# Router logits of seven chunks as multiply-and-sum on VectorE in place of flips and products on TensorE

## The chip, the cores and the metric

The kernel runs on one core of a Trainium2 chip. The metric is the device time of one execution in microseconds (us). TensorE (PE in the profile), VectorE (DVE), ScalarE (ACT), GpSimd (POOL) and SyncE (SP) each follow an instruction stream of their own and wait for each other by semaphores.

## The reference

Three layers in a row over 2304 tokens of 512 features, all in float32:

```python
scores = q @ k.T / 8 + bias            # 4 x 8 heads, causal, window of 128 tokens
x = softmax(scores) @ v                # attention
x = (h * clip(h + 3, 0, 6) / 6) @ w_out, with h = x @ w_in      # hard-swish layer
xn = x / (norm(x) + 1e-6)              # router
en = emb / (norm(emb) + 1e-6)          # 8 embeddings of 512
logits = xn @ en.T / tau
e = argmax(logits);  gate = softmax(logits)[e]
out = gate * (relu(x @ w1[e]) @ w2[e])                           # one expert per token
```

The change is in `logits` alone: eight sums of products of 512 per token.

## The kernel before, in words

The tokens go through attention and the hard-swish layer in nine chunks (`c`, 0 to 8) of 256, two tiles of 128 rows each. Attention runs in units of one chunk and one pair of heads, four units to a chunk; chunks 0 and 1 are `Early` units, the others `Unit`s. A `Unit` transposes its loaded keys and queries on VectorE (`kT`, `qT`, L567), scores them on TensorE (`sc_ps`, L583), finds the row limits and masks on VectorE (`soften`, L593 to L599), takes the exponential on ScalarE, scales on VectorE (`normalise`, L608 to L612), flips the weights on TensorE (`ps_pt`, L618), copies and masks them on ScalarE and GpSimd (`ph`, L625, L633) and multiplies by the values on TensorE (`acc`, L644). The attention of a chunk runs about two chunks ahead of its hard-swish layer.

The hard-swish layer of a chunk goes in eight steps `i` of 256 hidden features. Each has 24 products into `h_ps` (`gemm1`, L676), then `u` on ScalarE and VectorE (L686, L693), its split into `gh` on ScalarE and `gl` on VectorE (L155, L156), then 12 products into `y_ps` (`gemm2`, L719); products are made in three passes of split operands. In the chunks from 2 on, one step takes 1.91 of the planner's units of time, so a chunk takes 15.28.

When the last step of chunk `c` is done, its class `Route` begins: `rows` copies `y_ps` to two tiles `ys` and stores them; `flip` transposes each (`ps_y`, L747, 4 transposes a tile) and copies it to `yT` (L749); `norms` squares and sums the rows on ScalarE, in place, and takes a root on GpSimd (`rn`, L759); `logits` multiplies by the transposed embeddings `enT` (`lgT`, L766) and copies (L771); `total` adds the four parts (`lg`, L776); `choose` finds the expert on VectorE (L787 to L797); `ranks` counts earlier tokens of the same expert (`rk`, L802, L803); `place` computes a slot per token and scatters the row numbers to `slots` by two indirect DMAs on GpSimd (L818). After chunk 8 the experts run, with rows gathered by those slots.

The order of the work is fixed by `at(step, fn)`: all calls are sorted by their planned step, and TensorE executes its instructions in just that order. On the other engines a scheduler sorts the calls' instructions, and each engine then runs them in that order. SP issues nearly all loads and stores, one queue in order; the small loads `kr` and `qr` of keys and queries (L538) are 16 issues a unit. The pool `wp` has 17 buffers of 8 KB per partition; from the time that the weights of the hard-swish layer are all there, 16 of them hold these. The pool tag `f` has five buffers of 128x512.

The table `ROUTE` gives the steps of a chunk's `flip`, `norms`, `logits` and `ranks`, counted from the end of its last `gemm2`; its first row holds for chunks 0 to 6, its second for chunk 7. Chunk 8 has a schedule of its own.

Of the kernel before, what the change touches and what calls it, by code (L numbers as in the profile page):

```python
# [9 lines left out]
F32 = mybir.dt.float32  # L10
# [3 lines left out]
AF = mybir.ActivationFunctionType  # L14
ALU = mybir.AluOpType
# [42 lines left out]
P_BUFS, V_BUFS = 2, 2  # L58
FLIPS_AHEAD = 0.01

ROUTE = ((3.76, 4.57, 6, 8.46), (1, 1.43, 2.92, 4.5))

TOTAL = 0.95
PLACE_0 = (6.5, 10.6, 6.7, 2.08, 2.2, 1.0, 8.6)
# [27 lines left out]
def tile_kernel(  # L92
# [13 lines left out]
    nc = tc.nc  # L106
    B, H, S, D = q.shape
    NT, DM = out.shape
    DFF = w_in.shape[1] // 2
    NE = w1.shape[0]  # L110
# [3 lines left out]
    NCH = NT // CH  # L114
# [10 lines left out]
    dram = ctx.enter_context(tc.tile_pool(name="dram", bufs=1, space=bass.MemoryType.DRAM))  # L125
    main = ctx.enter_context(ExitStack())
    keep = main.enter_context(tc.tile_pool(name="keep", bufs=2))
    wp = main.enter_context(tc.tile_pool(name="wp", bufs=17))
# [8 lines left out]
    V = nc.vector  # L137

    def two_k(name, shape=(128, 512), dt=F32):
        return keep.tile(list(shape), dt, tag="f", bufs=5, name=name)  # L140

    def small(name, shape, dt=F32, bufs=2):
        return keep.tile(list(shape), dt, tag=name, bufs=bufs, name=name)
# [15 lines left out]
    def unit_of(head):  # L159
# [17 lines left out]
        out=whole, in_=whole, compare_op=ALU.is_ge, fill=MASKED, base=128, pattern=[[-1, 256]], channel_multiplier=1  # L177
    )
    nc.gpsimd.affine_select(
        out=whole, in_=whole, compare_op=ALU.is_ge, fill=MASKED, base=-1, pattern=[[1, 256]], channel_multiplier=-1  # L180
# [3 lines left out]
    for kinds in ((2, 2), (2, 0), (2, 1), (1, 2), (0, 2)):  # L184
        tables[kinds] = t = const.tile([128, 192], BF16, name="table%d%d" % kinds)
        for h, kind in enumerate(kinds):
            r = slice(64 * h, 64 * h + 64)
# [3 lines left out]


    ybuf = dram.tile([ROWS, DM], F32, name="ybuf")
    slots = dram.tile([NE * SLOTS, 2], I32, name="slots")

    pays = const.tile([128, NCH, 2, 2], I32, name="pays")
# [9 lines left out]
    units_of, half, share = fixed[:, 0:NP], fixed[:, NP:NP + 2], fixed[:, NP + 2:NP + 3]  # L206
# [7 lines left out]
        out=earlier, in_=earlier, compare_op=ALU.is_gt, fill=0.0, base=0, pattern=[[1, 128]], channel_multiplier=-1  # L214
# [5 lines left out]
        out=fold, in_=ident.rearrange("p (g e) -> p e g", g=KD)[:, 0:NE, :], axis=AX.X, op=ALU.add  # L220
# [38 lines left out]
    def embed():  # L259
        en = en_t.pop()[0:NE]  # L260

        junk = two_k("junk")
        n2 = small("n2", (NE, 1))
        nc.scalar.activation(out=junk[0:NE], in_=en, func=AF.Square, accum_out=n2)
        nc.gpsimd.tensor_tensor(out=n2, in0=n2, in1=half[0:NE, 0:1], op=ALU.pow)
        V.scalar_tensor_tensor(out=n2, in0=n2, scalar=1e-6, in1=rtau[0:NE], op0=ALU.add, op1=ALU.mult)
        V.reciprocal(out=n2, in_=n2)
        V.tensor_scalar(out=en, in0=en, scalar1=n2, scalar2=None, op0=ALU.mult)
        en_t.append(en)

    def turn_embed():
# [456 lines left out]
    class Route:  # L728
# [3 lines left out]
        def rows(self):  # L732
            c = self.c
            self.ss = small("ss", (128, 2))
            self.ys = []
            for t in range(2):
                ys = two_k("ys")
                nc.scalar.activation(out=ys, in_=y_t[c][t], func=AF.Copy, scale=1.0 / 6.0)
                r0 = c * CH + t * 128
                nc.sync.dma_start(out=ybuf[r0:r0 + 128, :], in_=ys)  # L740
                self.ys.append(ys)
            self.pay = pays[:, c]
# [11 lines left out]
        def norms(self):  # L754
            for t in range(2):
                ys = self.ys[t]
                nc.scalar.activation(out=ys, in_=ys, func=AF.Square, accum_out=self.ss[:, t:t + 1])
            self.rn = rn = small("rn", (128, 2))
            nc.gpsimd.tensor_tensor(out=rn, in0=self.ss, in1=half, op=ALU.pow)  # L759

        def logits(self):

            ps = bank([128, CH], "lgT")
            for t in range(2):
                for kk in range(KD):
                    nc.tensor.matmul(  # L766
                        ps[32 * kk:32 * kk + 32, t * 128:(t + 1) * 128], lhsT=enT[:, kk, :], rhs=self.yT[t][:, kk, :],
                        start=True, stop=True, skip_group_check=True,
                    )
            self.lgT = small("lgT", (128, CH), bufs=1)  # L770
            nc.scalar.copy(self.lgT, ps)  # L771
# [140 lines left out]
    def fetch(j, t):  # L912
        o, n = tiles_of(j)[t]
        xg = two_k("xg")
        ids, src = ids_t[j][0:n, t, 0:1], ybuf
        if j == 0 and o < EARLY:
            src = ybuf[0:NT - CH + 1, :]
            if t == 0:
                rows_t.append(small("rows", (128, n_first), I32))
            rows = rows_t[0][0:n, t:t + 1]  # L920
            V.tensor_scalar(out=rows, in0=ids, scalar1=NT - CH, scalar2=None, op0=ALU.min)
            ids = rows
        nc.gpsimd.indirect_dma_start(  # L923
            out=xg[0:n], out_offset=None, in_=src, in_offset=bass.IndirectOffsetOnAxis(ap=ids, axis=0)
        )
        xg_t[j, t] = xg
# [152 lines left out]
    def at(step, fn, *args):  # L1079
        todo[step].append((fn, args))  # L1080

    def begins(c, i=0):
        return FIRST_1[i] if c == 1 else FIRST[0] + FIRST[1] * (8 * (c - 2) + i)
# [5 lines left out]
    def ends(c, i=NF2 - 1):  # L1089
        return 0.0 if c == 0 else begins(c, i) + (SECOND_1 if c == 1 else FIRST[2])  # L1090
# [138 lines left out]
            at(begins(c, i), split_g, c, i)  # L1229
    for n in range(0, NT // 128, 3):  # L1230
        at(begins(BLANK[0] + n // 3, BLANK[1]), blank, n, n + 3)
    at(ROUTE[0][0] - 3.0, embed)
    at(ROUTE[0][0] - 0.3, turn_embed)
    for c in range(NCH - 1):
        r = Route(c)
        g = ends(c)
        d = ROUTE[c == NCH - 2]
        assert 0 < d[0] <= d[1] <= d[2] < d[2] + TOTAL < d[3]
        at(g, r.rows)
        at(g + d[0], r.flip, 0)  # L1240
        at(g + d[1], r.flip, 1)
        at(g + d[1], r.norms)
        at(g + d[2], r.logits)
        at(g + d[2] + TOTAL, r.total)
        at(g + d[2] + TOTAL, r.choose)
        at(g + d[3], r.ranks)
        at(g + d[3], r.place)
    g = begins(NCH - 1)
# [3 lines left out]
        pools["x"] = main.enter_context(tc.tile_pool(name="x2", bufs=1, side="right"))  # L1252

    at(g - 1, close_attention)
    assert g + PLACE_0[0] > ends(NCH - 2) + ROUTE[1][3]
    at(g + PLACE_0[0], rank_experts, False)
    at(g + PLACE_0[0], load_order, False, 0)
    at(g + PLACE_0[6], load_ids, 0, range(n_first))
# [9 lines left out]
    g = ends(NCH - 1)  # L1268
# [8 lines left out]
    r = Route(NCH - 1)  # L1277
# [14 lines left out]
    late = (n_first,)  # L1292
# [19 lines left out]
    for j in range(1, NE):  # L1312
# [6 lines left out]
        if j == 1:  # L1319
            s = PLACE_1  # L1320
            loads = [s[0] + s[1] * i for i in range(4)]
            splits = [s[2] + s[3] * i for i in range(8)]
            ids, gets, turns = LATE[0] + 0.05, [s[4] + s[5] * t for t in range(n)], [s[8] + s[9] * t for t in range(n)]
        else:
            s = [x + b - 16 for x in NEXT]
            s[5], s[7], s[9] = NEXT[5], NEXT[7], NEXT[9]
            loads = [s[0], s[1], s[2], s[3]]
# [39 lines left out]
    with tc.If(n_rounds > 0):  # L1367
        with ExitStack() as rest:
# [15 lines left out]
            def overflow(j, r):  # L1384
# [16 lines left out]
                for n in range(NT // 128):  # L1401
                    rows = f2.tile([128, DM], F32, tag="rows", name="rows_r")
                    nc.sync.dma_start(out=rows, in_=ybuf[n * 128:(n + 1) * 128, :])
                    hot = f2.tile([128, 128], F32, tag="hot", name="hot")
                    V.tensor_scalar(
                        out=hot, in0=wanted, scalar1=-128.0 * n, scalar2=down_p, op0=ALU.add, op1=ALU.is_equal
                    )
                    for kk in range(KD):
                        nc.tensor.matmul(
                            ps[:, kk, :], lhsT=rows[:, kk * 128:(kk + 1) * 128], rhs=hot,  # L1410
                            start=(n == 0 and kk == 0), stop=(n == NT // 128 - 1 and kk == KD - 1),
                            skip_group_check=True,
                        )
# [19 lines left out]
                for n in range(NT // 128):  # L1433
                    rows = f2.tile([128, DM], I32, tag="rows", name="rows_r")
                    nc.sync.dma_start(out=rows, in_=out[n * 128:(n + 1) * 128, :].bitcast(I32))
                    hot = f2.tile([128, 128], F32, tag="hot", name="hot")
                    V.tensor_scalar(
                        out=hot, in0=across, scalar1=128.0 * n, scalar2=whose, op0=ALU.add, op1=ALU.is_equal
                    )
                    moved = pf.tile([128, DM], F32, tag="moved", name="moved")  # L1440
                    nc.tensor.matmul(moved, lhsT=hot, rhs=ob, start=True, stop=True)
                    theirs = pf.tile([128, DM], F32, tag="theirs", name="theirs")
                    nc.tensor.matmul(theirs, lhsT=hot, rhs=all_one, start=True, stop=True)
                    mine = f2.tile([128, DM], I32, tag="mine", name="mine")
                    V.tensor_copy(out=mine, in_=theirs)
                    V.copy_predicated(rows, mine, moved.bitcast(I32))
                    nc.sync.dma_start(out=out[n * 128:(n + 1) * 128, :].bitcast(I32), in_=rows)
# [35 lines left out]
```

## Time and profile before

| what | value |
|---|---|
| median of 3 runs (lowest, highest) | 789.95 us (789.27, 791.37) |
| profiled execution: its own time | 795.89 us |
| profiled execution: span from first to last instruction | 793.9 us |
| mean granted clock of TensorE in it | 0.992 of full speed |
| TensorE busy | 769.2 us, 97% of the span |
| VectorE busy | 454.7 us, 57% |
| ScalarE busy | 400.5 us, 50% |
| GpSimd busy | 177.1 us, 22% |
| attention and hard-swish layer, to chunk 8's end | about the first 575 us |
| experts | the rest |

The profiled execution is one of its own, 5.94 us (0.75%) above the median of the runs. Times within the trace are counted from the start of the span. Busy shares over the whole span mix stages: VectorE, for example, has slices at nine tenths in the first 100 us and slices at four to six tenths later. Matmuls are pipelined, so that rows of a TensorE timeline overlap, and what a group costs in a full stream is read from its start to the next group's start.

### The profile page before, as it was taken

The page shows a single profiled execution, that of the slowest core. Times are in us where ns is not written, and L with a number is a line of the kernel's source. Part 1 is how long each engine was busy: PE and PEld are TensorE (multiplying, and loading weights), DVE is VectorE, ACT ScalarE, POOL GpSimd, SP SyncE. Part 2 cuts the span into 40 slices and gives each one's busy share as a digit, 9 for nine tenths or more (in the row PEclk, how much of TensorE's full clock was granted, in tenths as well). Part 3 has the DMA queues.
Part 4 walks back from the last instruction along what each step waited for, and adds up shares of the span by engine and source line. Part 5 has one row for each costly group of instructions (what it writes and reads, how often), then busy time and mean ns, then how long its engine had stood idle before and what let it go on. Part 6 is the DMA issues. An engine that isn't in the chain of part 4 may idle for free. (4 is left out here: it accounts for less than half of the span.)

```text
span 793.9 us, 16238 instructions
## 1 busy us (share of the span) xinstructions
PE 769.2 (97%) x5970; PEld 677.6 (85%) x5970; DVE 454.7 (57%) x1272; ACT 400.5 (50%) x941; POOL 177.1 (22%) x357
## 2 busy tenths in 40 slices
PE   7999999999999999999999999999989999999995
PEld 5666577788888898898988888888989999999994
DVE  2799987656565555646456453237827537546621
ACT  5898655455454454455454452426525535544510
POOL 4000003222221312313232322013123122133210
PEclk9999999999999999999999999999999999999998
DMA  9954522422333232242323110048268465456200
GB/s 258 338 179 111 176 49 48 54 61 47 77 80 78 39 67 74 37 96 46 74 61 59 52 52 1 28 93 294 94 206 269 149 219 194 149 201 216 82 26 27
DMA packets 157077, 88.51 MB, mean 111 GB/s; under 512 B 119187, under 2 KB 135699, under 8 KB 156992
## 3 DMA queue, kind: packets, MB, share of 16 engines
q1 hardware_dynamic: 153248, 77.84, 35.9%
q0 software_dynamic: 3744, 9.58, 3.5%
q8 instruction: 49, 0.80, 0.5%
q14 instruction: 36, 0.29, 0.2%
HBM read 73.03 MB, written 14.46 MB: 110 GB/s over the span
## 5 line engine op out<-in xcount | busy, mean ns | idle before, releaser
L676 PEld LDWEIGHTS h_ps<-xs,w_i 128*128 128x128 f32 x1536 | 192.1, 192 | 6.4 <-issue 2.0
L676 PE MATMUL h_ps<-xs,w_i 128*128 128x256 f32 x1536 | 196.1, 284 | 0.0
L719 PE MATMUL y_ps<-w_o,gh 128*128 128x512 f32 x512 | 163.5, 400 | 1.0 <-ACT gh L155 0.9
L686 ACT ACTIVATE u<-h_ps,three 128x512 f32<-128x512 f32 x72 | 49.4, 687 | 126.4 <-PE h_ps L676 101.3
L719 PEld LDWEIGHTS y_ps<-w_o,gh 128*128 128x128 f32 x512 | 91.5, 188 | 24.8 <-issue 7.0
L633 POOL TENSOR_SCALAR_AFFINE_SELECT ph<-ph 64x128 f32<-64x128 f32 x224 | 78.1, 349 | 141.3 <-ACT ph L625 88.7
L693 DVE SCALAR_TENSOR_TENSOR u<-u,h_ps 128x512 f32<-128x512 f32 x72 | 49.4, 685 | 104.3 <-ACT u L686 103.9
L965 PE MATMUL ps_u<-x,w_e 128*128 128x280 f32 (+5 forms) x768 | 105.0, 293 | 0.0
L719 PE MATMUL y_ps<-w_o,gl 128*128 128x512 f32 x256 | 100.5, 393 | 0.4 <-DVE gl L156 0.4
L965 PEld LDWEIGHTS ps_u<-x,w_e 128*128 128x128 f32 x768 | 100.2, 188 | 0.2
L156 DVE TENSOR_TENSOR w_e<-st,w_e 128x1024 fp32r<-128x1024 f32 x64 | 76.5, 1217 | 38.2 <-ACT w_e L155 38.2
L989 PE MATMUL ps_o<-hs,w_e 128*128 128x280 f32 (+4 forms) x576 | 79.9, 299 | 0.0
L989 PEld LDWEIGHTS ps_o<-hs,w_e 128*128 128x128 f32 x576 | 78.0, 192 | 0.0
L155 ACT CAST w_e<-st 128x1024 fp32r<-128x1024 f32 x64 | 65.5, 1049 | 17.1 <-DMA st<-in_moe_w_dram 6.2
L156 DVE TENSOR_TENSOR gl<-u,gh 128x512 fp32r<-128x512 f32 x64 | 45.8, 715 | 37.1 <-ACT gh L155 37.1
L602 ACT ACTIVATE pt<-pt,nm 128x128 f32<-128x128 f32 x112 | 44.1, 394 | 31.3 <-DVE pt L599 29.9
L719 PEld LDWEIGHTS y_ps<-w_o,gl 128*128 128x128 f32 x256 | 48.0, 188 | 12.0 <-DVE gl L156 1.5
L1064 POOL DMA_INDIRECT out_dram<-ob,ids x23 | 30.3, 1317 | 116.4 <-DVE ob L1063 105.9
L155 ACT CAST gh<-u 128x512 fp32r<-128x512 f32 x64 | 39.6, 619 | 22.3 <-DVE u L693 22.2
L973 ACT ACTIVATE hs<-ps_u 128x280 fp32r<-128x280 f32 (+5 forms) x64 | 25.6, 403 | 44.9 <-PE ps_u L965 44.2
L974 DVE SCALAR_TENSOR_TENSOR hs<-ps_u,hs 128x280 fp32r<-128x280 f32 (+5 forms) x64 | 27.9, 442 | 20.1 <-ACT hs L973 19.8
L818 POOL DMA_INDIRECT slots<-pays,dest x18 | 19.9, 1104 | 84.6 <-DVE u L693 52.1
(180 smaller groups left out, 1021.6 us busy)
## 6 DMA issues: line engine op xcount, KB each, us to landing
st<-in_moe_w_dram SPq DMA_DIRECT2D x32, 512.0 KB
st<-in_moe_w_dram SPq DMA_DIRECT2D x16, 1024.0 KB
wst<-in_moe_w_in_dram SPq DMA_DIRECT2D x8, 1024.0 KB
wst<-in_moe_w_out_dram SPq DMA_DIRECT2D x8, 1024.0 KB
ybuf<-ys SPq DMA_DIRECT2D x18, 256.0 KB
out_dram<-empty SPq DMA_DIRECT2D x18, 256.0 KB
kr<-in_k_dram SPq DMA_DIRECT2D x48, 48.0 KB
vr<-in_v_dram SPq DMA_DIRECT2D x24, 96.0 KB
```

Source lines behind the costliest of these rows:

```text
L155: nc.scalar.copy(hi, src)
L156: eng.tensor_tensor(out=lo, in0=src, in1=words(hi), op=ALU.subtract)
L602: nc.scalar.activation(out=x, in_=x, func=AF.Exp, scale=-1.0, bias=nm[:, j:j + 1], accum_out=sums[h][:, j:j + 1])
L633: nc.gpsimd.affine_select(out=out, in_=x, compare_op=ALU.is_gt if out is prev else ALU.is_ge, fill=0.0, base=0, pattern=[[0, 2], [-1 if ou ...
L676: nc.tensor.matmul(hp[:, f, :], lhsT=w[:, a, kk, f * 128:(f + 1) * 128], rhs=xs[:, b, kk, :], start=(n == 0), stop=(n == 3 * KD - 1),)
L686: nc.scalar.activation(out=u, in_=hp, func=AF.Relu, bias=three, scale=1.0)
L693: V.scalar_tensor_tensor(out=u, in0=u, scalar=6.0, in1=h_t[c, i], op0=ALU.min, op1=ALU.mult)
L719: nc.tensor.matmul(y_t[c][t], lhsT=g[a][:, f, t * 128:(t + 1) * 128], rhs=w[:, b, f, :], start=(i == 0 and f == 0 and n == 0), stop=(i == ...
L965: nc.tensor.matmul(ps, lhsT=w[:, a, kk, (f % 2) * 128:(f % 2) * 128 + 128], rhs=x[:, b, kk, c0:c1], start=(n == 0), stop=(n == 3 * KD - 1),)
L974: V.scalar_tensor_tensor(out=hs[:, 1, f, c0:c1], in0=ps, scalar=0.0, in1=words(hs[:, 0, f, c0:c1]), op0=ALU.max, op1=ALU.subtract)
L989: nc.tensor.matmul(ps, lhsT=ws_t[j, 4 + f // 2][:, a, f % 2, d * 128:(d + 1) * 128], rhs=hs[:, b, f, 0:width(j)], start=(n == 0), stop=(n ...
L1064: x = nc.gpsimd.indirect_dma_start(out=out, out_offset=bass.IndirectOffsetOnAxis(ap=ids[0:n, t, 0:1], axis=0), in_=ob[0:n], in_offset=None ...
```

## The change

For chunks 0 to 6 `flip`, `logits` and `total` are no longer called. The eight normalised embeddings are written once to `en_rows` in DRAM. Per chunk, two loads (`spread`, 1 MB each) copy four of them to every partition, into the free buffer of `wp`, under the name `en_all`; both go through the same buffer one after the other, and both are on SP. `dots` then makes one `tensor_tensor_reduce` per embedding and tile on VectorE, 16 a chunk: `ys` times the embedding, elementwise, with the sum along the row into `lg`, and the products into a tile `junk` that nothing reads. `norms` puts its squares into the same `junk`, since `ys` must live on, and comes right after `rows`. `choose`, `ranks` and `place` follow at 10.9 and 12.28 steps after the chunk's end, where it was 6.95 and 8.46. Chunk 0's part is 4.0 steps later than the others'. `enT` is still made, for chunks 7 and 8, which are as before.

```diff
-ROUTE = ((3.76, 4.57, 6, 8.46), (1, 1.43, 2.92, 4.5))
+ROUTE = (1, 1.43, 2.92, 4.5)
+DOTS = ((-3.5, 4.5), (0.8, 1.0), (7.4, 0.8), 10.9, 12.28)
+EMBED = 4.0
...
+    en_rows = dram.tile([NE, DM], F32, name="en_rows")
...
         V.tensor_scalar(out=en, in0=en, scalar1=n2, scalar2=None, op0=ALU.mult)
+        nc.sync.dma_start(out=en_rows, in_=en)
...
         def norms(self):
             for t in range(2):
                 ys = self.ys[t]
-                nc.scalar.activation(out=ys, in_=ys, func=AF.Square, accum_out=self.ss[:, t:t + 1])
+                to = self.junk if self.c < NCH - 2 else ys
+                nc.scalar.activation(out=to, in_=ys, func=AF.Square, accum_out=self.ss[:, t:t + 1])
...
+        def spread(self, half):
+            self.en = wp.tile([128, NE // 2, DM], F32, tag="w", name="en_all")
+            src = en_rows[NE // 2 * half:NE // 2 * (half + 1), :].rearrange("(o e) d -> o (e d)", o=1)
+            nc.sync.dma_start(out=self.en.rearrange("p e d -> p (e d)"), in_=src.to_broadcast([128, NE // 2 * DM]))
+
+        def dots(self, e):
+            if e == 0:
+                self.lg = small("lg", (128, 2, NE))
+            for t in range(2):
+                V.tensor_tensor_reduce(
+                    out=self.junk, in0=self.ys[t], in1=self.en[:, e % (NE // 2), :],
+                    scale=1.0, scalar=0.0, op0=ALU.mult, op1=ALU.add, accum_out=self.lg[:, t, e:e + 1],
+                )
...
-    at(ROUTE[0][0] - 3.0, embed)
-    at(ROUTE[0][0] - 0.3, turn_embed)
+    at(EMBED - 3.0, embed)
+    at(EMBED - 0.3, turn_embed)
...
-        d = ROUTE[c == NCH - 2]
+        at(g, r.rows)
+        if c < NCH - 2:
+            at(g + 0.3, r.norms)
+            loads, *halves, d2, d3 = DOTS
+            late = EMBED if c == 0 else 0.0
+            for x in range(2):
+                at(g + loads[x] + late if c or x else 2.0, r.spread, x)
+            for e in range(NE):
+                x, y = divmod(e, NE // 2)
+                at(g + halves[x][0] + halves[x][1] * y + late, r.dots, e)
+            at(g + d2 + late, r.choose)
+            at(g + d3 + late, r.ranks)
+            at(g + d3 + late, r.place)
+            continue
+        d = ROUTE
```

How the instructions stand in the two programs is shown at three places. The first is TensorE in the hard-swish layer of chunk 3, where chunk 2's logits were made; `h_ps` and `y_ps` are the two products of the layer. Before:

```order
L719 MATMUL y_ps<-w_o,gl 128x512
L766 MATMUL lgT<-yT,enT 32x128 x8
L676 MATMUL h_ps<-xs,w_i 128x256 x24
L776 MATMUL lg<-fold,lgT 128x8 x2
L719 MATMUL y_ps<-w_o,gh 128x512 x2
L719 MATMUL y_ps<-w_o,gl 128x512
```

Now:

```order
L723 MATMUL y_ps<-w_o,gh 128x512 x2
L723 MATMUL y_ps<-w_o,gl 128x512
L680 MATMUL h_ps<-xs,w_i 128x256 x24
L723 MATMUL y_ps<-w_o,gh 128x512 x2
L723 MATMUL y_ps<-w_o,gl 128x512
```

`lgT` and `lg` are gone and nothing stands in their place; the two groups of flips before them are gone in the same way, and `rk` stands later, again right ahead of a `ps_pt`.

The second place is VectorE in the same chunk, in the attention unit beside the second half of chunk 2's dots. `pt` and `rs` are the unit's weights and row scales; a dot is the row L777 with `junk`, followed by a row that reads the sum out. Before, from the last L593 of the unit's `soften` to the end of its `normalise`:

```order
L593 ISA pt,nm<-sc_ps,table_100 128x192
L593 ISA nm 128x1
L567 STREAM_TRANSPOSE kT<-kr 128x384
L599 TENSOR_TENSOR pt<-pt 128x2x64
L608 TENSOR_SCALAR rs<-sums_150 128x2
L567 STREAM_TRANSPOSE qT<-qr 128x256
L609 RECIPROCAL rs<-rs 128x2
L612 TENSOR_SCALAR pt<-pt,rs 128x128 x2
```

Now:

```order
L777 ISA junk,lg<-ys,en_all 128x512
L777 ISA lg 128x1
L603 TENSOR_TENSOR pt<-pt 128x2x64
L612 TENSOR_SCALAR rs<-sums_151 128x2
L777 ISA junk,lg<-ys,en_all 128x512
L777 ISA lg 128x1
L613 RECIPROCAL rs<-rs 128x2
L571 STREAM_TRANSPOSE kT<-kr 128x384
L616 TENSOR_SCALAR pt<-pt,rs 128x128 x2
L612 TENSOR_SCALAR rs<-sums_152 128x2
```

Of the eight dots of this half, one stands ahead of the first half of `normalise`, one inside it and one inside the second half; the other five stand after it, two ahead of the next `u`, two between `u` and `gl` and one behind `gl`.

The third place is VectorE in chunk 1's hard-swish layer, beside the first half of chunk 0's dots. Before, across a unit's `soften` and `normalise`:

```order
L599 TENSOR_TENSOR pt<-pt 128x2x64
L608 TENSOR_SCALAR rs<-sums_150 128x2
L609 RECIPROCAL rs<-rs 128x2
L612 TENSOR_SCALAR pt<-pt,rs 128x128 x2
L813 TENSOR_TENSOR to<-rk,oh 128x16
L816 TENSOR_TENSOR seen<-seen,oh 128x8
```

Now, at the same unit, from `soften`'s last row on:

```order
L603 TENSOR_TENSOR pt<-pt 128x2x64
L777 ISA junk,lg<-ys,en_all 128x512
L777 ISA lg 128x1
L697 SCALAR_TENSOR_TENSOR u<-u,h_ps 128x512
L777 ISA junk,lg<-ys,en_all 128x512
L777 ISA lg 128x1
L612 TENSOR_SCALAR rs<-sums_151 128x2
L612 TENSOR_SCALAR rs<-sums_152 128x2
```

Three dots stand ahead of these rows, within `soften`, and three more behind them, two of them behind a `gl`, before the first `L616` of `normalise`: eight dots in all, together with a `u` and a `gl`, which stood behind `normalise` before. Chunk 0's `choose`, which stood ahead of this unit's `soften`, has moved behind the second half of the dots. That half stands in the same way around the `soften` and `normalise` of the unit after the next: eight dots, a `u` and a `gl`, and there a `kT` too, ahead of the last rows of `normalise`.

## Rows read from the trace of the kernel before

**Rows 1.** The page, busy time of each engine over the span:

```profile
PE 769.2 (97%) x5970; PEld 677.6 (85%) x5970; DVE 454.7 (57%) x1272; ACT 400.5 (50%) x941; POOL 177.1 (22%) x357
```

**Rows 2.** Busy by stretch: PE, PEld, DVE, ACT, POOL; then clock, DMA share, GB/s:

```profile
103.50:155.00 51.50, 49.28 (x427) 41.30 (x426) 35.63 (x137) 29.15 (x84) 13.47 (x36) 0.97 0.32 52
238.00:293.50 55.50, 55.50 (x495) 49.06 (x494) 31.30 (x121) 27.44 (x78) 14.27 (x36) 1.00 0.32 63
```

**Rows 3.** Timeline of TensorE: start, duration, engine, line, operation, count:

```profile
182.48 0.60 PE L747 MATMUL ps_y<-ident,ys 128*128 128x128 f32 x4
...
216.85 0.60 PE L618 MATMUL ps_pt<-ident,pt 128*128 128x128 f32 x4
...
230.20 0.60 PE L618 MATMUL ps_pt<-ident,pt 128*128 128x128 f32 x4
...
232.19 0.73 PE L719 MATMUL y_ps<-w_o,gh 128*128 128x512 f32 x2
...
237.92 0.60 PE L747 MATMUL ps_y<-ident,ys 128*128 128x128 f32 x4
238.28 0.71 PE L719 MATMUL y_ps<-w_o,gh 128*128 128x512 f32 x2
...
249.39 0.64 PE L766 MATMUL lgT<-yT,enT 128*32 128x128 f32 x16
249.97 3.14 PE L676 MATMUL h_ps<-xs,w_i 128*128 128x256 f32 x24
252.95 0.51 PE L776 MATMUL lg<-fold,lgT 128*128 128x8 f32 x4
253.31 0.71 PE L719 MATMUL y_ps<-w_o,gh 128*128 128x512 f32 x2
...
273.00 0.89 PE L644 MATMUL acc<-ph,vr 64*64 64x192 f32 x24
...
460.43 0.60 PE L747 MATMUL ps_y<-ident,ys 128*128 128x128 f32 x4
```

**Rows 4.** Groups of VectorE by line and shape: busy, mean ns, idle before:

```profile
L156 DVE TENSOR_TENSOR gl<-u,gh 128x512 fp32r<-128x512 f32 x64 | 45.8, 715 | 37.1 <-ACT gh L155 37.1
L320 DVE SCALAR_TENSOR_TENSOR w<-wst,w 128x1024 int32<-128x1024 int32 x16 | 19.4, 1218 | 0.1
L458 DVE CUSTOM_DVE_ANT_0 pt<-sc_ps,table 128x256 f32<-128x256 f32 x24 | 9.3, 417 | 0.0
```

**Rows 5.** Timeline of VectorE in a unit without routing; in brackets the idle time before:

```profile
220.23 0.34 DVE L593 CUSTOM_DVE_ANT_0 pt<-sc_ps,table 128x192 f32<-128x192 f32 x1
...
221.97 0.57 DVE L567 STREAM_TRANSPOSE kT<-kr 128x384 f32<-128x384 f32 x1
...
224.14 0.48 DVE L612 TENSOR_SCALAR pt<-pt,rs 128x128 f32<-128x128 f32 x2
225.56 0.69 DVE L693 SCALAR_TENSOR_TENSOR u<-u,h_ps 128x512 f32<-128x512 f32 x1 [0.93 <-ACT u L686]
```

**Rows 6.** Timeline of TensorE in chunk 1's layer:

```profile
129.60 3.12 PE L676 MATMUL h_ps<-xs,w_i 128*128 128x256 f32 x24
...
135.83 0.73 PE L719 MATMUL y_ps<-w_o,gh 128*128 128x512 f32 x2
...
138.97 0.60 PE L618 MATMUL ps_pt<-ident,pt 128*128 128x128 f32 x4
...
152.31 3.63 PE L676 MATMUL h_ps<-xs,w_i 128*128 128x256 f32 x24
...
161.40 0.60 PE L618 MATMUL ps_pt<-ident,pt 128*128 128x128 f32 x4
```

**Rows 7.** Timeline of GpSimd behind a chunk's scatter:

```profile
270.20 2.44 POOL L633 TENSOR_SCALAR_AFFINE_SELECT ph<-ph 64x128 f32<-64x128 f32 x7 [6.81 <-DMA slots<-pays,dest]
```

**Rows 8.** Timeline of SP's queue, the issues of one unit's queries:

```profile
207.44 7.29 SPq L538 DMA_DIRECT2D qr<-in_q_dram  x8
```

More of the change, by code (lines that the diff above doesn't have):

```diff
@@ L735, in rows @@
             self.ys = []
+            if c < NCH - 2:
+                self.junk = two_k("junk")
             for t in range(2):
@@ L1236, in tile_kernel @@
         g = ends(c)
-        d = ROUTE[c == NCH - 2]
+        at(g, r.rows)
+        if c < NCH - 2:
+            at(g + 0.3, r.norms)
[11 more added lines that the diff above has]
+        d = ROUTE
         assert 0 < d[0] <= d[1] <= d[2] < d[2] + TOTAL < d[3]
-        at(g, r.rows)
         at(g + d[0], r.flip, 0)
@@ L1254, in tile_kernel @@
     at(g - 1, close_attention)
-    assert g + PLACE_0[0] > ends(NCH - 2) + ROUTE[1][3]
+    assert g + PLACE_0[0] > ends(NCH - 2) + ROUTE[3]
     at(g + PLACE_0[0], rank_experts, False)
```

## The prediction

> **What bounds the kernel now.** I read the busy shares first: TensorE is at 97% of the span, VectorE at 57%, ScalarE at 50%, GpSimd at 22% [rows 1]. Then the table of busy time by stretch, since shares mix stages. In chunk 3's layer TensorE is busy in all 55.50 of 55.50 us at full clock, VectorE in 31.30; in chunk 1's layer TensorE has 2.2 us of gaps in 51.5 and VectorE is at 35.63, with the clock at 0.97 [rows 2]. So from chunk 2's layer on an instruction taken from TensorE shortens the path by its own length as long as the others keep up, and in chunk 1's layer the others already don't quite. The third view is TensorE's timeline, for the price of what goes.
>
> **Removed from TensorE.** Two groups of flips, `lgT` and `lg` per chunk. Chunk to chunk I take the first flip of chunk 1 (182.48) and that of chunk 6 (460.43): 277.95 us over five chunks, 55.59 each [rows 3]. A unit without routing lasts from 216.85 to 230.20, 13.35 us; four make 53.40 [rows 3]. The difference, 2.19, is what routing costs a chunk; `rk` stays and I leave it 0.06 of that, a guess from its two small products. So 2.13 a chunk, and **6 x 2.13 = 12.8 us** for chunks 1 to 6, whose flips begin at the six ends of those five periods. Read from start to next start, the groups themselves are 0.36 for a flip, 0.58 for `lgT` and 0.36 for `lg` (from 237.92, 249.39 and 252.95); with the second flip like the first that is 1.66 a chunk, 10.0 for six [rows 3]. The rest sits in neighbours that run a little slower beside them. I take 12.8 and keep 10.0 as the lower end. Chunk 0's four groups are worth 2.1 at the same price.
>
> **Added to VectorE.** No row shows this instruction on two float32 tiles of SBUF. Nearest are `gl`, two such inputs of the same shape without a sum, 715 ns; and the custom form with a sum in `soften`, 417 for half the elements, so at most 834 [rows 4]. I take 0.72 us, since `gl` has the same shape: 16 x 0.72 = 11.5 a chunk, VectorE 42.8 of the new 53.5. The ends are 0.65 and 0.83.
>
> Is 80% too full for an engine that works in order? In a steady unit `soften` starts at 220.23, the last scaled weights are done at 224.62 (224.14 + 0.48) [rows 5], and their flip is at 230.20 [rows 3]: 5.6 us of slack. In the new order three dots stand ahead of the end of `normalise`, 2.2 us, which leaves 3.4. The next `u`, at 225.56 [rows 5], has five dots ahead of it, 3.6 us; behind it come two dots and `gl`. The normalised weights at about 226.8, two dots (1.4), `u` (0.7), two dots (1.4) and `gl` (0.7) end by 231.0; the `y_ps` group that asks for it starts at 232.19 with two products that don't need it, 0.6 us [rows 3]. So in chunks 1 to 6 I price the dots at **nothing**, with 1.8 us of cover left per half chunk; seven dots stand before that `gl`, so 0.26 us more for each would use it up.
>
> **Chunk 0's dots** lie in chunk 1's layer, and there eight of them, a `u` and a `gl` stand ahead of the end of one unit's `normalise`. `soften` to `normalise` takes 4.4 us in a unit, of which about 1.0 is transposes [rows 5]; with 8 x 0.72 and 1.4 it becomes some 10.6. In the first such unit the scores end at 129.6 and `soften` begins 0.4 later; ready at 140.6 on the old clock, where the flip stood at 138.97: 1.6 late, part of it already at the `y_ps` of 135.83, which waits for that `gl` [rows 6]. In the second, scores end at 152.31 and a `kT` of 0.57 [rows 5] stands ahead too: ready at 163.9, flip at 161.40, 2.5 late [rows 6]. Together 4.1 us of new waits against 2.1 removed: **+2.0**. The ends: -2.1 if the dots run while VectorE would have waited for ScalarE, and +5 if the waits also push the loads and `u`s behind them (half as much again, about, plus the earlier `norms` on ScalarE in that crowded stage).
>
> **Moved, and cheap.** `choose` to `place` come 3.82 steps later, which is a unit (13.35 us), so `rk` and the scatter find the same neighbours. ScalarE loses three copies a chunk and is not on the path. The seven chunks' 14 loads are 1 MB each: the stretch moves 63 GB/s with the DMA engines busy 0.32 of the time [rows 2], so alone about 63 / 0.32 = 197 GB/s and at most 5.3 us a load, twice in 53 us. They go into the one buffer of `wp` that no weight holds. They share SP's queue with the key and query loads: a unit's queries take 7.29 us to issue from 207.44 [rows 8], and the keys issued ahead of them are first used at 221.97 [rows 5], so there are about 7 us between the last issue and the use. One more issue and 5.3 us fit in.
>
> **The sum.** -12.8 + 2.0 = -10.8 on the profiled execution, 795.89 to 785.1. That execution lies 5.94 us above the median of the runs; the same difference from 789.95 gives **779.2**.
>
> **Rivals.**
> *The dot runs at half rate.* Then it costs what 1024 elements cost now, 1.22 us [rows 4]; 16 make 19.5, and VectorE has 50.8 of 53.5 us. The five dots ahead of `u` go from 3.6 to 6.1 us, the two ahead of `gl` from 1.4 to 2.4, so with the 0.5 more of each of seven dots (3.5 us) the 1.8 us of cover per half become about 2 us of wait: 12 halves x 2 = 24, chunk 0 another 6 beyond its 2.0, together -10.8 + 30, some 809, **slower**. It decides from about 1.0 us a dot. Against it: L320, two 4-byte inputs from SBUF, shows 1.19 ns an element like `gl` at 1.40 with its fixed part, so two inputs alone don't halve [rows 4]; but it makes no sum. The Trainium skill, in "Vector Engine (DVE) Microarchitecture Reference", section "Points that are easy to get wrong", states that a scalar-tensor-tensor form with two non-bf16 sources in SBUF runs at half throughput, for want of a read port for the accumulator. By that rule this rival would be the forecast; L320 is of that form and speaks against it, as far as it goes. Chance 0.08.
> *The big loads hold up keys and queries.* SP works in order, and a load that waits for its buffer (the second half may not start before the first four embeddings are done) keeps all behind it. Beyond about 5 us of such hold (7 less some 2 for the small loads to land, an estimate), every further us stops `kT` and, a unit later, TensorE. With 1.5 us at each of 14 loads: 21, so about 800, **slower**. For it: one queue for everything. Against: the table of the schedule asks for the buffer 0.7 steps after its last reader. Chance 0.08.
> *The scatter lands late.* GpSimd waits 6.81 us for `slots` and then has 2.44 us of masks, done at 272.64 [rows 7]; their `acc` is at 273.00 [rows 3]. Only 0.36 us lie between. If VectorE, fuller now, hands over the slots 1 us later, TensorE waits 0.6 in each of six chunks, and with shorter units ahead perhaps 1: 4 to 6 us given back, **784**. Against: no dot stands between `rk` and `dest`. Chance 0.15.
>
> **How the numbers follow.** My forecast has 0.69, and a range of its own of 775 to 784: the lower end from chunk 0's -2.1 (789.95 - 14.9), the upper from 10.0 in place of 12.8 and chunk 0 near its +5. The range of eight in ten, 774.5 to 789, takes in the scatter and leaves out the two slow rivals. About 0.3% (2.4 us) is what a measurement of this kernel can tell from no change: faster is below 787.6, slower above 792.3. Faster: 0.69 + 0.10 of the scatter's chance = 0.79. Same: 0.05 of the scatter (a later hand-over than I priced) and 0.02 of the loads = 0.07. Slower: 0.08 + 0.06 = 0.14.
>
> **What would show it.** In the new profile: the mean of a dot near 0.72 us (1.2 would be the first rival); TensorE at 53.5 us per chunk and without gaps in chunk 3's layer, VectorE near 43 there; one or two waits of TensorE for `pt` or `gl`, 4 us in all, in chunk 1's layer; SP's loads still some 7 us ahead of `kT`; `acc` not waiting for `ph`. I am wrong if the period of the steady chunks stays above 54.5 us, or if waits in chunk 1's layer exceed 8 us.

## The result, and the profile after

The changed kernel takes 781.41 us (median of 4 runs, 780.51 to 782.86) against 789.61 us: a ratio of 0.9894, with a 95% interval of 0.9869 to 0.9918. That is faster by 8.2 us, where 10.8 were forecast. Two later comparisons of the same two kernels gave 0.9905 (0.9883 to 0.9927) and 0.9878 (0.9858 to 0.9898). So the kernel is faster by 7.5 to 9.7 us by the three ratios; the forecast of 10.8 lies over all three, and inside the interval of the last alone.

The page of the changed kernel, busy time of the engines, the group of the dots, and the line of the big loads (count, KB each, median us from issue to landing):

```profile
PE 753.5 (97%) x5774; PEld 663.7 (85%) x5774; DVE 516.9 (66%) x1496; ACT 392.1 (50%) x920; POOL 186.4 (24%) x357
...
L777 DVE CUSTOM_DVE_ANT_0 junk<-ys,en_all 128x512 f32<-128x512 f32 x112 | 77.2, 689 | 20.5 <-DMA en_all<-en_rows 10.9
...
en_all<-en_rows SPq DMA_DIRECT2D x14, 1024.0 KB, 4.9
```

TensorE lost 15.7 us of work, VectorE gained 62 [rows 1]; a dot takes 689 ns, a load lands in 4.9 us. What came of it is seen by stretch. The table of busy time by stretch of the changed kernel (start to end, length, then busy us of PE, PEld, DVE, ACT, POOL, granted clock, DMA share, GB/s), for chunk 1's layer and for chunk 3's:

```profile
105.30:174.50 69.20, 65.36 (x556) 55.73 (x555) 55.08 (x206) 37.61 (x108) 17.85 (x46) 1.00 0.43 105
...
227.95:281.50 53.55, 53.55 (x468) 47.63 (x468) 40.58 (x155) 26.43 (x75) 15.42 (x35) 1.00 0.48 119
```

In chunk 3's layer TensorE is still busy all the time and VectorE has 40.6 us of work instead of 31.3 [rows 2], where 42.8 were forecast. In chunk 1's layer TensorE has gaps of 3.8 us.

The steady chunks can be summed exactly from TensorE's timeline. Before, from the first steady flip (174.75) to chunk 7's transposes (506.59):

```profile
174.75 0.60 PE L618 MATMUL ps_pt<-ident,pt 128*128 128x128 f32 x4
...
506.59 1.03 PE L747 MATMUL ps_y<-ident,ys 128*128 128x128 f32 x8
```

and in the changed kernel:

```profile
174.50 0.60 PE L622 MATMUL ps_pt<-ident,pt 128*128 128x128 f32 x4
...
493.72 1.04 PE L753 MATMUL ps_y<-ident,ys 128*128 128x128 f32 x8
```

331.84 against 319.22 us: 12.6 less, or 2.1 for each of six chunks. Cut at the same points, the spans of the profiled executions in this study (each is one execution) give this table; the layer of chunk 1 is counted from TensorE's first `h_ps<-xs` to the first steady flip.

| kernel | until chunk 1's layer | chunk 1's layer | steady, to chunk 7's flips | to the end |
|---|---|---|---|---|
| before | 103.97 | 70.78 | 331.84 | 287.3 |
| before, again (e1) | 103.38 | 67.93 | 331.84 | 288.2 |
| before + 14 loads (e3) | 104.00 | 70.97 | 332.09 | 285.7 |
| before + 12 loads (e7) | 104.03 | 67.57 | 331.84 | 282.9 |
| changed | 105.32 | 69.18 | 319.22 | 286.9 |
| changed, again (e5) | 103.37 | 69.22 | 319.25 | 284.5 |
| changed, third (e10) | 104.00 | 69.17 | 320.70 | 287.4 |
| 24 dots (e4) | 104.19 | 69.20 | 319.94 | 285.2 |
| 32 dots (e6) | 104.00 | 69.25 | 344.12 | 285.5 |
| chunk 0 old (e2) | 104.02 | 68.03 | 319.60 | 285.9 |
| chunk 0 old, again (e9) | 103.86 | 68.53 | 319.27 | 289.1 |
| chunk 0 old + its loads (e11) | 103.60 | 68.11 | 319.65 | 285.4 |
| chunk 0 old + idle dots (e12) | 104.09 | 70.35 | 319.24 | 286.1 |

The steady column is the same within 1.5 us for kernels with the same work in it; the first and the last column vary by 2 and 6 us with no tie to the edit. e8, which changes chunk 7 as well, is left out of the last two columns; its first two are 104.08 and 68.37. The reader should take causes from the two middle columns, and the size of the whole from the runs.

### The profile page after: what moved, and what is told of

Same layout as the page of the kernel before. It is cut to its first block, busy times and chain, and to the rows that moved or that the text cites. A ratio compares the mean times of both kernels' runs of the same rounds, so it can differ in the third digit from the quotient of the medians.

```text
span 780.6 us, 16081 instructions
## 1 busy us (share of the span) xinstructions
PE 753.5 (97%) x5774; PEld 663.7 (85%) x5774; DVE 516.9 (66%) x1496; ACT 392.1 (50%) x920; POOL 186.4 (24%) x357
## 4 chain that ended last, share of the span: by engine, by line
PE 65%; DMA 9%; DVE 9%; issue 8%; ACT 5%; POOL 3%; SPq 1%; POOLq 0%; DVEq 0%; ACTq 0%
PE y_ps L723 20%; PE h_ps L680 20%; PE ps_u L986 6%; PE ps_z L1068 3%; PE acc L648 3%; PE ps_o L1010 3%; DMA st<-in_moe_w_dram 2%; PE sc_ps L587 2%; DMA ids<-slots 2%; DMA out_dram<-ob,ids 2%; PE ps_pt L622 2%; DMA xg<-ybuf,ids 2%; PE y_ps L714 1%; PE h_ps L667 1%; POOL xg L944 1%
## 5 line engine op out<-in xcount | busy, mean ns | idle before, releaser
L637 POOL TENSOR_SCALAR_AFFINE_SELECT ph<-ph 64x128 f32<-64x128 f32 x224 | 89.0, 397 | 196.7 <-ACT ph L629 152.7
L777 DVE CUSTOM_DVE_ANT_0 junk<-ys,en_all 128x512 f32<-128x512 f32 x112 | 77.2, 689 | 20.5 <-DMA en_all<-en_rows 10.9
```

The lines of the kernel that those rows point to most:

```text
L637: nc.gpsimd.affine_select(out=out, in_=x, compare_op=ALU.is_gt if out is prev else ALU.is_ge, fill=0.0, base=0, pattern=[[0, 2], [-1 if ou ...
L777: V.tensor_tensor_reduce(out=self.junk, in0=self.ys[t], in1=self.en[:, e % (NE // 2), :], scale=1.0, scalar=0.0, op0=ALU.mult, op1=ALU.add ...
```

## The experiments

The theory: TensorE sets the time of the steady chunks, so its removed products are the gain, and VectorE's dots hide; chunk 0's dots lie in a crowded stage and give some back. The rivals: the loads hold up keys and queries or disturb something; VectorE is already on the path; the scatter is late.

**e1, e5, e10: both kernels again.** The first profiled execution had been 5.94 us over the median of its kernel, so both were profiled anew.

> The kernel before, unchanged, to see what a second profile of it shows. The first profiled execution took 795.89 us where its runs had a median near 789.6. Theory A (one slow execution, the time lies ahead of chunk 1's layer or in the experts): the runs stay at 789 to 791, the period of a chunk stays 55.6 us, and a second profile within 2 us of 790 shows the stretch from chunk 7's flips to the end, or the one up to chunk 1's layer, shorter by 4 to 6 us than in the first (287.3 and 98 us there). Rival (profiling itself stretches this kernel by 6 us but not the changed one): the second profile is again near 796.

The runs: 791.82 us (789.61 to 793.38), ratio to before 0.9997 (0.9978 to 1.0015). The profiled execution took 793.38 us, 1.6 above the median of its runs: not 796 again, as the rival has it, but not within 2 us of 790 either. It shows chunk 1's layer in 67.93 us instead of 70.78. So theory A was wrong about the place: the 2.85 us lie in that layer, not ahead of it or in the experts. There the first trace has, on ScalarE and on TensorE:

```profile
146.37 0.69 ACT L686 ACTIVATE u<-h_ps,three 128x512 f32<-128x512 f32 x1 [1.76 <-remote]
```

```profile
148.03 0.53 PE L618 MATMUL ps_pt<-ident,pt 128*128 128x128 f32 x2 [0.96 <-DVE pt L612]
```

and a granted clock of 0.83 in the ten us from 145: it is at 0.50, the lower level, from about 150 to 153.5. The row of the whole layer in that trace:

```profile
103.97:174.75 70.78, 68.56 (x585) 58.88 (x583) 46.27 (x172) 38.09 (x107) 16.31 (x44) 0.98 0.32 58
```

In the second trace `u` waits 0.75 us for its products there, the clock stays at 1.00, neither wait is there, and TensorE has 66.75 us of work and 1.15 of gaps. So of the 2.85 us, 1.8 are the same work at a lower clock and 1.1 are waits. The fair base for chunk 1's layer is 67.6 (e7) to 67.9.

> The changed kernel, unchanged, on the chip and in the call of the next three. If the traces' sum holds (-12.6 in chunks 1 to 6, +1.2 in chunk 1's layer against the second profile of before, nothing elsewhere): 11 us under before, ratio near 0.986. If the first measurement was the true one (0.9894): 8 to 9 us under it, and a place must then be found where the changed kernel loses 3 us more than these two terms.

> The changed kernel once more, for its spread of 778 to 785 us in e5: theory A, the stretches outside the steady chunks vary from run to run (the way to chunk 1's layer by 2 us, the experts by 5 in the traces so far), median 780 to 783 and a trace that adds up as before: 69.2 us in chunk 1's layer, 319.2 us from there to chunk 7's flips. Rival: chunk 1's layer itself is longer in the slow runs (a fall of the granted clock there, as in the first profile of before); a trace of such a run would show 71 us or more there.

782.38 us (778.02 to 784.75) and 782.76 us (780.75 to 783.38). Both traces add up as the first did, 69.2 us in chunk 1's layer and 319 to 321 from there. The ratios 0.9905 and 0.9878 don't reach the 0.986 that the sum of the traces asks for (12.6 less 1.3 is 11.3 us; the runs say 7.5 to 9.7). No execution with a slower layer was caught, so the rival of e10 has no support; but some 2 to 3 us of the difference between traces and runs stay unexplained. They aren't shown to belong to the change: e4, further down, has all of its work and more, and its runs are 10.6 us faster, which is what its own trace asks for (331.84 less 319.94 is 11.9, less 1.3); the intervals overlap.

**e2, e9: chunk 0 the old way,** with the old first row of the table, (3.76, 4.57, 6, 8.46), as `ROUTE_0`.

```diff
-        if c < NCH - 2:
+        if 0 < c < NCH - 2:
...
-        d = ROUTE
+        d = ROUTE if c else ROUTE_0
```

> The changed kernel with chunk 0's logits made the old way (flips and products on TensorE), chunks 1 to 6 as changed. By the two traces chunk 0's part of the change is worth 1.6 us (chunk 1's layer, from y_ps of chunk 0 to the first steady flip, is that much shorter), so this should be 1 to 2 us slower than the changed kernel, 782 to 784. By the prediction's own price of chunk 0's dots (+2.0) it should be 2 us faster, 779. Within 1 us of the changed kernel would mean that chunk 0's dots give back just what they remove.

780.0 us (778.11 to 780.43), ratio 0.9854 (0.9834 to 0.9875). I had put 782 to 784 from the first two traces, whose base had the slow layer in it, and missed; against the second trace of before it should have been 1.3 us faster than the changed kernel, and that is what the layer shows: 68.0 against 69.2.

> The kernel of e2 again (chunk 0 the old way), beside the changed kernel in the next run, on one chip and in one call. By the traces chunk 1's layer is 1.2 us shorter here (68.0 against 69.2 us from its first product to the first steady flip) and all else is alike: 1 to 2.5 us faster than the changed kernel. If chunk 0's dots were worth their removal: no faster than it.

780.63 us (778.83 to 783.16) beside 782.76 for the changed kernel: 0.9856 (0.9834 to 0.9879) against 0.9878. Chunk 1's layer takes 68.53 us here. Chunk 0's part of the change, dots and loads together, costs 0.7 to 1.2 us by the traces and 2 by the runs, over and above the products that it replaces. The intervals overlap, so this version is the better one by the trace and by two medians, and not beyond doubt.

**e4, e6: more dots.** How much of VectorE is still free in the steady chunks? Half of the embeddings (e4, below) or all (e6, with `if self.c:`) are multiplied twice, in chunks 1 to 6; the second sums go to a tile that nothing reads.

```diff
+                if self.c and e % 2 == 0:
+                    V.tensor_tensor_reduce(
+                        out=self.junk, in0=self.ys[t], in1=self.en[:, e % (NE // 2), :],
+                        scale=1.0, scalar=0.0, op0=ALU.mult, op1=ALU.add, accum_out=self.more[:, t, e:e + 1],
+                    )
```

> The changed kernel with 24 dots instead of 16 in each of chunks 1 to 6 (every second embedding twice, the second sum into a tile that nothing reads). A dot's pitch is 0.61 us in the trace, so a half chunk gets 2.4 us more of VectorE. If the cover of the steady chunks is some 2.6 us per half chunk (the predicted 1.8, widened by seven dots at 0.61 instead of 0.72): within 2 us of the changed kernel, 780 to 783, no waits for gl or pt of more than 0.5 us in chunk 3's layer. If VectorE were already on the path there: 0.6 us or more per half chunk, 12 halves, 789 or more.

780.44 us (779.73 to 781.51), ratio 0.9866 (0.9843 to 0.9889): half as many dots again cost nothing. (The pitch of 0.61 us holds where another instruction follows the dot; a second dot right behind it starts 0.73 us later. Four dots more are 2.4 to 2.9 us.) The same stretch of chunk 3's layer in its trace:

```profile
226.80:280.30 53.50, 53.50 (x468) 47.58 (x467) 44.70 (x170) 26.54 (x75) 15.53 (x33) 1.00 0.50 115
```

> The changed kernel with every dot of chunks 1 to 6 made twice: 32 a chunk, 9.8 us more of VectorE, some 52 us in a period of 53.4. My theory (cover of about 2.6 us per half chunk, half chunks get 4.9 more): TensorE waits some 2 us per half chunk, 12 halves, 800 to 810 us, and the waits are for gl and pt. If the scheduler's order spreads them well enough: 785 to 795. No change (within 2 us of the changed kernel) would mean that my reading of the cover is wrong by a factor of two.

803.2 us (801.07 to 804.7), ratio 1.0159 (1.0138 to 1.0181). So with 32 dots the cover is gone and the change would have been a loss: 344.1 us for the steady chunks, 24.9 more than in the changed kernel, 4.15 for each of six. The size is as expected, but it is made up in another way. The row of the steady chunks, and two waits from TensorE's timeline:

```profile
173.25:517.37 344.12, 329.70 (x2763) 290.62 (x2762) 291.88 (x1068) 151.94 (x425) 110.24 (x207) 0.98 0.36 90
```

```profile
216.47 0.17 PE L829 MATMUL rk<-oh,earlier 128*128 128x16 bf16 x1 [5.86 <-DVE oh L820]
...
335.44 0.19 PE L829 MATMUL rk<-oh,earlier 128*128 128x16 bf16 x1 [2.29 <-ACT sh L825]
```

It isn't `gl` or `pt` that is late but `rk`: the ranks stand at a fixed place of TensorE's order, and the dots push `choose`, which makes `oh` and `sh`, past it. TensorE's gaps are 14.4 us, 13.5 of them ahead of five `rk`. The other 10.5 us are longer busy time for the same products: the granted clock is 0.50 in three stretches, from about 215.6 to 222.4, 335.0 to 341.9 and 451.1 to 454.5, each of which begins within 1 us of the end of one of the three longest waits for `rk` (5.86, 2.29 and 2.26 us). That waits and clock together come to about the 24 us which I had expected of waits alone is luck. In the changed kernel no `rk` waits.

**e3, e7: the loads alone,** in the kernel before; e7 has `0 < c < NCH - 2`, so chunk 0's two are left out.

```diff
+        if c < NCH - 2:
+            for x in range(2):
+                at(g + (-3.5, 4.5)[x] + (4.0 if c == 0 else 0.0) if c or x else 2.0, r.spread, x)
```

> The kernel before with the 14 loads of 1 MB added at the changed kernel's steps, on the same queue into the same buffer, and nothing that reads them. If the loads cost nothing (my theory): 788 to 791, the time of the kernel before. If loads beside small key and query loads hold up the units (the rival of the prediction), or disturb the experts: 1 to 4 us slower, which would be what is missing between 12.8 and the measured 8.2.

794.11 us (791.18 to 795.17), ratio 1.0036 (1.0019 to 1.0052): 14 loads that nobody reads cost some 3 us, beyond the interval. The trace has them in chunk 1's layer, 70.97 us against 67.57 in e7 below, where TensorE's gaps are 3.6 us against 1.3. The longest wait is at the place that was slow in the first trace of before as well:

```profile
147.49 0.69 ACT L688 ACTIVATE u<-h_ps,three 128x512 f32<-128x512 f32 x1 [2.66 <-remote]
```

The flip behind it comes 1.59 us late for `pt`; two groups of scores wait 0.38 and 0.47 us for a scaled `qT`. Here the clock stays at 1.00. No transpose of a key or a query waits for its load in that layer. The steady chunks take 332.1 us, as without the loads.

> The kernel before with the 12 big loads of chunks 1 to 6 only, without chunk 0's two, which run beside chunk 1's layer. With all 14 loads the kernel before was 0.36% slower, and its trace showed the 3 us in chunk 1's layer. If the cost is that stage's alone: the time of before (ratio 0.998 to 1.0015). If big loads cost wherever they run: still 2.5 to 3 us slower.

789.95 us (787.52 to 792.18), ratio 1.0 (0.9986 to 1.0014). Twelve of the loads cost nothing, so the rival that they hold up keys and queries falls for the steady chunks. In chunk 1's layer the trace of e3 doesn't show it either, since no transpose waits for a load there; what the two loads cost in e3 is of another kind, and open.

**e11, e12: chunk 0's loads and dots apart,** in the kernel of e2. The edit of e11 comes first, then that of e12, whose dots multiply one tile of `ys` by the other and put the sums where nothing reads them.

```diff
+        if c == 0:
+            for x in range(2):
+                at((2.0, 8.5)[x], r.spread, x)
```

```diff
+        if c == 0:
+            for e in range(NE):
+                x, y = divmod(e, NE // 2)
+                at(DOTS[1 + x][0] + DOTS[1 + x][1] * y + 4.0, r.idle_dots, e)
```

> The kernel of e2 with chunk 0's two big loads put back and nothing that reads them. If the loads are what chunk 0's part costs (as e3 against e7 says: 3 us in chunk 1's layer): 2 to 3 us slower than e9, chunk 1's layer near 71 us. If it is the dots on VectorE, as I predicted: within 1 us of e9, 68 us.

> The kernel of e2 with 16 idle dots of chunk 0 (one tile of rows times the other, sums that nothing reads) at the changed kernel's steps, without the loads. Without a load to wait for the scheduler spreads them further forward. If VectorE's time is the cost: 2 us or more slower than e9, waits for pt in chunk 1's layer. If it is the loads, or the place that they force on the dots: within 1 us of e9.

e11: 781.5 us (778.51 to 783.35), ratio 0.9872 (0.9851 to 0.9892); chunk 1's layer 68.1 us, as in e2 and e9 (68.0 and 68.5). e12: 782.5 us (781.33 to 784.16), ratio 0.9883 (0.9864 to 0.9903); the layer takes 70.35 us, 1.8 more than in e9. Its row, and the longest wait on TensorE:

```profile
104.09:174.44 70.35, 67.87 (x585) 58.73 (x584) 55.20 (x206) 39.68 (x111) 19.55 (x46) 0.98 0.38 73
```

```profile
128.28 0.43 PE L623 MATMUL ps_pt<-ident,pt 128*128 128x128 f32 x2 [1.05 <-DVE pt L617]
```

The next flip waits 0.77 us more for `pt`, and a `y_ps` at 112.58 0.56 for `gl`. So dots without loads do make TensorE wait, at other places than in the changed kernel. But its gaps are 2.5 us in all, against 2.0 in e9. The larger part of the 1.8 us is busy time for the same products, 67.9 us against 66.6: behind the two waits for `pt` the granted clock is 0.50 from about 130.8 to 134.2. In the changed kernel's traces it stays at 1.00 in this layer, so e12 shows that the dots are felt there, and not what they cost in the changed kernel; the runs, 1.9 us over e9 and so between the two expectations, have overlapping intervals. For the loads the runs don't agree: 3 us in e3, about 1 in e11 (within its interval), none in e11's trace. What decides between them is open.

**e8: chunk 7 by dots too.** Chunk 8's layer has no attention beside it, and VectorE is busy about half of the time there (24.3 of 46.4 us in e2's trace).

```diff
+DOTS_7 = ((-3.5, 1.9), (0.4, 0.35), (3.4, 0.25), 4.4, 4.9)
-            loads, *halves, d2, d3 = DOTS
+            loads, *halves, d2, d3 = DOTS if c < NCH - 2 else DOTS_7
```

> Chunk 0's logits the old way, chunks 1 to 6 as changed, and chunk 7's by dots too, with its own steps (both halves between 0.4 and 4.2 steps after its end, choose at 4.4). In chunk 8's layer no attention runs and VectorE is busy about a third of the time; TensorE is full. If TensorE's products are what counts there too: 2 us less than e2, 778. If chunk 7's choose comes later than the experts' ranking wants it (its second load must wait for the first half's dots): the ranking and the first rows come late, 780 to 784.

784.86 us (782.97 to 785.6), ratio 0.993 (0.9915 to 0.9946), 0.8% slower than e2. The second expectation has the direction, and falls 0.9 us short in size:

```profile
506.88 0.19 PE L825 MATMUL rk<-oh,earlier 128*128 128x16 bf16 x1 [3.77 <-DVE oh L816]
```

But its reason doesn't: no dot of chunk 7 waits for a load. The sixteen dots, with `u` and `gl` between them, keep VectorE from 491.0 to 505.3; `oh` comes at 506.64, where it was 503.06 in e2, and TensorE's order holds `rk` ahead of the experts' ranking. From about 505.4 to 512.2, beginning within that wait of 3.77 us, the granted clock is 0.50. Flips and products cost TensorE more, and give the answer sooner.

## Why the prediction was right

**The steady chunks.** 6 x 2.13 = 12.8 us was the term; 12.6 are measured, with a chunk at 53.5 us. Pricing the removed groups by the difference of two periods [rows 3], and not by their own length (10.0), was worth 2.6 us of accuracy.

**The dots.** Taken at 0.72 us, measured 0.689; the next instruction starts about 0.61 us after a dot does, and the next dot 0.73. The half-rate rival is out: the form makes its sum at the pace of `gl` [rows 4]. On the rule of the Trainium skill ("Vector Engine (DVE) Microarchitecture Reference", section "Points that are easy to get wrong") the trace says that this form, with two float32 tiles of SBUF and a sum, isn't halved; L320 had hinted at that. "Nothing" in chunks 1 to 6 is shown twice: no wait in the trace, and no cost for 8 dots more (e4). My 1.8 us of cover per half chunk was too small: four dots more, 2.4 to 2.9 us, fitted.

**Chunk 0.** The term was +2.0, from 4.1 of new waits and 2.1 removed. The gaps and the clock of 0.97 that I read in this stage [rows 2] were in good part those of the one slow execution (e1). By the rows of chunk 1's layer, against the second trace of before, whose row of the same table is

```profile
103.40:171.30 67.90, 66.75 (x584) 57.58 (x583) 46.17 (x172) 37.99 (x107) 16.49 (x44) 1.00 0.32 60
```

TensorE's gaps grew from 1.15 to 3.84 us, 2.7 more, and its work shrank by 1.4: +1.3. The sign and the stage are right; both halves of the term came out a third smaller than forecast, and that they shrank alike is luck, since the waits are other ones. TensorE's timeline of the changed kernel in that layer, its longest waits:

```profile
129.73 0.88 PE L587 MATMUL sc_ps<-kT,qT 64*64 64x192 f32 x16 [0.87 <-ACT qT L578]
...
142.02 0.88 PE L587 MATMUL sc_ps<-kT,qT 64*64 64x192 f32 x16 [0.90 <-ACT qT L578]
...
160.75 0.53 PE L622 MATMUL ps_pt<-ident,pt 128*128 128x128 f32 x2 [0.87 <-DVE pt L616]
```

I had the flip of the first unit 1.6 late; it isn't late at all (138.53 + 0.87 for the last weights, flip at 139.71), and the `gl` ahead of it costs 0.29. The second unit's flip is 0.87 late instead of 2.5. The other two of the longest waits are for `qT`, which the prediction left out. On VectorE, from the first dot on, and then on ScalarE:

```profile
131.48 0.69 DVE L777 CUSTOM_DVE_ANT_0 junk<-ys,en_all 128x512 f32<-128x512 f32 x1
...
138.53 0.87 DVE L616 TENSOR_SCALAR pt<-pt,rs 128x128 f32<-128x128 f32 x4
...
140.39 0.43 DVE L571 STREAM_TRANSPOSE qT<-qr 128x256 f32<-128x256 f32 x1
```

```profile
129.17 0.51 ACT L578 ACTIVATE qT<-qT,fixed 128x256 f32<-128x256 f32 x1
...
141.45 0.52 ACT L578 ACTIVATE qT<-qT,fixed 128x256 f32<-128x256 f32 x1
```

For the second wait, at 142.02, the eight dots hold back the next unit's transposes; their scaling on ScalarE, at 141.45, comes behind the copies of `ph` and a `gh`, and the next scores wait. In the second trace of before that scaling starts at 136.62 and the scores at 139.64. The first wait, at 129.73, is no dot's doing: it comes ahead of the first dot, at 131.48. `qT` is transposed at 127.36, but in ScalarE's order its scaling now stands behind both copies of `ph` and behind `part`, a copy that waits for `acc`; in the second trace of before it stands between the two copies of `ph`. So 0.87 of the new waits come from another order on ScalarE and not from VectorE's time.

**The other rivals.** The scatter: masks done at 278.38 + 3.30 = 281.68, `acc` at 282.05, 0.37 us of slack as before [rows 3, 7]. At the same chunk the second trace of the changed kernel has 0.01 us of slack, and in the third `acc` waits 0.58 us; the other five chunks have over 1 us in all three. So it is near, and costs at most that much, not the 4 to 6 us of the rival. The loads: 4.9 us to land, and no transpose waits for a key or query in the steady chunks; VectorE waits four times for `en_all` (10.9 us in all), and has the time.

**The total.** -12.6 + 1.3 = -11.3 by the traces, -10.8 forecast, -8.2 measured, and -7.8 and -9.0 in the medians of the two repeats. The large term stands with its mechanism, and the small one with its sign; the traces' sum overstates the runs by some 2 to 3.5 us. The last column of the table alone varies by 6 us from execution to execution, but no experiment here shows that the difference lies there.

## What to carry to other kernels

Work moved from a full engine to a half-idle one is worth its price by the period, not by its own length, and hides as long as the other engine's order leaves cover; find out how much by adding more of it (here 8 dots more per chunk were free, 16 more cost some 21 us in all, part of it in waits and part in the lower clock that followed them). What such work delays first need not be the result of the step beside it: follow what stands behind it in the queue, here the next unit's transposes and a fixed place in TensorE's order; and compare the order on the engines that were not meant to change, here ScalarE. In a stage that is already crowded, and where only the answer's delay counts, leave it where it was: chunk 0 done the old way is 0.7 to 2 us better, chunk 7 by dots 0.8% worse.

## What the runs showed of the hardware

GpSimd pays for the dots. Its eight masks of a unit took, in the changed kernel, without and with dots beside them (a `gl` runs beside them in both cases):

```profile
256.83 3.30 POOL L637 TENSOR_SCALAR_AFFINE_SELECT ph<-ph 64x128 f32<-64x128 f32 x8 [10.94 <-ACT ph L629]
...
283.05 4.79 POOL L637 TENSOR_SCALAR_AFFINE_SELECT ph<-ph 64x128 f32<-64x128 f32 x8
```

and the mean of all 224 went from 349 to 397 ns. The Trainium skill, in "SBUF — State Buffer", section "SBUF: two separate sides", has a VectorE instruction with two SBUF inputs and a GpSimd instruction that reads SBUF block each other on a shared pair of ports. The trace agrees, with 1.5 us more beside four dots. The seven masks behind a scatter, 2.44 us before [rows 7], took 3.30 with a dot at 280.84 among them; that the slack stayed at 0.37 us there is owed to a wait for `slots` of 5.95 instead of 6.81 us.

The same program had two lengths of one stage in two executions: 70.8 and 67.9 us for chunk 1's layer of the kernel before. The longer one had a wait of ScalarE that the profile puts down to "remote" (1.76 us; 2.66 in e3), and behind it a granted clock of 0.50, the level of 1.2 GHz and not of 2.4, for 3.4 us, after TensorE had waited 0.96 us for `pt` and 0.41 for `ph`. What "remote" stands for here is left open.

The clock makes a wait dearer than its length, but not each time. It fell to 0.50 with or behind waits for `rk` of 5.86, 2.29 and 2.26 us in e6 and of 3.77 in e8, and behind two waits of 1.05 and 0.77 us in e12. It stayed at 1.00 with 1.59 us in e3, 1.60 and 1.48 in e6, and with the waits of 0.87 and 0.90 in the changed kernel. What it answers to is left open.
